# Uncast fp32 output stores on Sync's queue, and column halves for fewer weights and output blocks, in an attention plus soft-MoE kernel

## The chip, the cores and the metric

The kernel runs on one core of a Trainium2 chip. The metric is device time in microseconds of one execution, and less is better. Before the change the median of five runs is 190.15 us (189.98 to 190.43). The profile is that of one further execution, which took 189.8 us; its span, from the first to the last profiled instruction, is 188.0 us.

Five engines work beside each other, each in the order of its own program: PE (matrix multiply), DVE (vector), ACT (activation), POOL (GpSimd) and SP (Sync). Data moves between memory and the on-chip buffer SBUF by DMA, which an engine issues and 16 shared transfer engines carry out. A DMA that changes the data type goes through GpSimd's queue in this kernel.

## The reference

Attention with a sliding window for heads 0 to 3 and a dilated one for heads 4 to 7 gives `x` with 4608 rows and 512 columns. A soft mixture of experts follows:

```python
logits = x @ phi                                  # 4608 x 32
d = np.exp(logits - logits.max(0, keepdims=True)); d /= d.sum(0, keepdims=True) + 1e-09
slot_input = (d.T @ x).reshape(E, S_per_e, D)     # 8 experts, 4 slots each
for e in range(E):
    slot_out[e] = np.maximum(slot_input[e] @ w1[e], 0.0) @ w2[e]
c = np.exp(logits - logits.max(1, keepdims=True)); c /= c.sum(1, keepdims=True) + 1e-09
return (c @ slot_out.reshape(n_slots, D)).astype(np.float32)
```

`w1` is 8 x 512 x 1024 and `w2` is 8 x 1024 x 512, both fp32. Inputs and output are fp32; on the chip the arithmetic has fp16 operands and fp32 sums.

## The kernel before

The kernel has two parts. The first goes over the eight batches. For each it loads q, k and v, computes both kinds of attention, and from the result the exponentials of the logits (`ET`, 32 slots by 4608 rows, in four copies of which one lies on each quarter of the partitions) and the slot inputs. All of q, k, v and the weights are loaded by GpSimd's DMAs, which turn fp32 into fp16 on the way. The order of the instructions is written out by hand (`prologue`, `slot0`, `slot1`, `slot2`).

The weights' loads are issued between those of the attention: `weights` (L464) is called twice per batch. It issues w1 two at a time by `load_w1` (L194), and then w2 by `load_w2` (L198). `load_w2(e)` loads all of an expert's w2 in one DMA, whose pieces in memory are 8 KB (four rows of 512 fp32). `load_w2(e, half)` loads the left or right 256 columns in two DMAs, whose pieces are 1 KB. Experts 0, 1, 5 and 2 come whole; the experts of `HALVED` (3, 4, 6, 7) come as left halves first, then as right halves. Experts 5, 6 and 7 reuse buffers of the attention, so their loads wait until the last batches have let these go.

The second part begins when all batches are through. The slot inputs are multiplied by w1 (L620), go through ReLU and are transposed (L627 to L637). Then `slot_out` (L653) multiplies by w2, one half of the columns at a time, eight matmuls per expert and half, into `so[half]`, and after the last expert ACT copies the sum to `so_sb[half]` as fp16 (L665). `combine(half, pair)` (L669) makes two blocks of 128 output rows of one half of the columns: two matmuls of 256 columns each into a PSUM tile, then the scaling by `rrow` (one over the row sum of c), which moves the data to the fp16 tile `ot` in SBUF. Even pairs are scaled by ACT in two instructions (L685), odd pairs by DVE in one (L689). A GpSimd DMA then stores the tile, and turns fp16 to fp32 on the way (L695). There are 18 pairs of blocks for each half, thus 36 stores of 256 KB. The pool has 24 `ot` buffers (`NFIN // 2 + 6`), and PSUM has four for `combine`.

The main sequence (L700 to L710) takes the left half of all experts, the right half of the four whole ones, then the 18 left pairs; after pairs 5, 9 and 13 it puts in the right half of experts 3, 4 and 6, then that of 7, and then come the 18 right pairs. Since GpSimd issues stores as well as loads, all stores stand behind all loads in its queue. Sync issues nothing but the loads of the masks (L438) and of the identity matrix (L439) at the start; at the end it waits for every outstanding DMA, and a barrier over all engines (L742) closes the program.

Of the kernel before, what the change touches and what calls it, by code (L numbers as in the profile page):

```python
# [9 lines left out]
FP32 = mybir.dt.float32  # L10
FP16 = mybir.dt.float16
U32 = mybir.dt.uint32
AF = mybir.ActivationFunctionType
ALU = mybir.AluOpType
# [10 lines left out]
DMODEL = H * D  # L25
# [15 lines left out]
NFIN = N_ROWS // 128  # L41
UNITS = 7
NH = DMODEL // 2


def make_masks():
# [19 lines left out]
def kernel(  # L66
# [10 lines left out]
    nc = tc.nc  # L77
# [6 lines left out]
    consts = ctx.enter_context(tc.tile_pool(name="consts", bufs=1))  # L84
# [8 lines left out]
    ET = consts.tile([128, N_ROWS + 64], FP16, name="ET")  # L93
# [1 line left out]
    rcol = consts.tile([128, N_SLOTS], FP32, name="rcol")  # L95
    siTm = consts.tile([128, 4, E_EXP, N_SLOTS], FP16, name="siTm")
    rrow = consts.tile([128, NFIN], FP32, name="rrow")
    so_sb = [consts.tile([128, NH], FP16, name=f"so_sb{i}") for i in range(2)]

    w1_pool = ctx.enter_context(tc.tile_pool(name="w1p", bufs=1))  # L100
    w2a_pool = ctx.enter_context(tc.tile_pool(name="w2a", bufs=1))
# [21 lines left out]
    def slab_weights(e, tag, n):  # L123
        t = fix.tile([128, n], FP16, name=f"w2_{e}", tag=tag)
        w2t[e] = t[:, 0 : 8 * DMODEL].rearrange("p (c n) -> p c n", c=8)
# [68 lines left out]
    def load_w1(e, i):  # L194
        src = moe_w1[e].rearrange("(c p) f -> p c f", p=128)
        nc.gpsimd.dma_start(out=w1t[e][:, 2 * i : 2 * i + 2, :], in_=src[:, 2 * i : 2 * i + 2, :])  # L196

    def load_w2(e, half=None):  # L198
        if half is None:
            nc.gpsimd.dma_start(  # L200
                out=w2t[e].rearrange("p (h l) n -> p h (l n)", h=2),
                in_=moe_w2[e].rearrange("(h p l) n -> p h (l n)", h=2, l=4),
            )
            return
        src = moe_w2[e].rearrange("(h p l) n -> h p l n", h=2, l=4)
        c0 = NH * half
        for h in range(2):
            nc.gpsimd.dma_start(  # L208
                out=w2t[e][:, 4 * h : 4 * h + 4, c0 : c0 + NH], in_=src[h][:, :, c0 : c0 + NH]
            )  # L210
# [253 lines left out]
    def weights(b, g):  # L464
        if b < B - 2:
            if g == 1 or b > 0:
                load_w1(*next_w1.pop(0))
        elif b == B - 2:
            if g == 0:
                while next_w1:  # L470
                    load_w1(*next_w1.pop(0))
                load_w2(0)
                load_w2(1)
            else:
                slab_weights(5, "v2", V_SLAB)
                load_w2(5)
        elif g == 0:
            raw_pool.release()
            vs_pool.release()
            pool = tc.alloc_tile_pool(name="w2b", bufs=1, side="right")  # L480
            late_pools.append(pool)
            for e in (2, 3, 4):
                w2t[e] = pool.tile([128, 8, DMODEL], FP16, name=f"w2_{e}", tag=f"w2_{e}")
            slab_weights(6, "qk0", QK_SLAB)
            load_w2(2)
            for e in HALVED[:3]:
                load_w2(e, 0)
        else:
            slab_weights(7, "v0", V_SLAB)
            load_w2(7, 0)  # L490
            for e in HALVED:
                load_w2(e, 1)

    HALVED = (3, 4, 6, 7)
    late_pools = []

    def slot0(b):
        att, b1, b2, b3 = b < B, b - 1 >= 0 and b <= B, 2 <= b < B + 2, b + 1 < B
        if att:
            qk_dil(1, b, 1)  # L500
            emit_scores(b, 0)
            if b + 2 < B:
                load_qk(0, b + 2)
                load_qk(1, b + 2)
            weights(b, 0)
# [28 lines left out]
    def slot1(b):  # L534
        att, b1, b3 = b < B, 1 <= b <= B, b + 1 < B
        if b3:
            qk_plain(0, b + 1)
        if att:
            emit_scores(b, 1)
            if b + 2 < B:  # L540
                load_v(b + 2)
            weights(b, 1)
            emit_av(b, "p", 0)
            emit_norm(b, "p", 0)
        if b1:
            back_xT_dil(b - 1, 0)
        if b3:
            qk_plain(1, b + 1)
        if att:
            emit_av(b, "p", 1)  # L550
            emit_norm(b, "p", 1)
        if b1:
            back_xT_dil(b - 1, 1)
# [35 lines left out]
    xT_pool.release()  # L589
    x_pool.release()  # L590
    h_pool = tc.alloc_tile_pool(name="hp", bufs=1)
    out_pool = tc.alloc_tile_pool(name="outp", bufs=NFIN // 2 + 6)


    psum_so = tc.alloc_tile_pool(name="psum_so", bufs=1, space=bass.MemoryType.PSUM)
# [2 lines left out]
    for g in range(4):  # L598
# [8 lines left out]
        out=diag,  # L607
        in0=UT[:, 0:4, :].rearrange("p c (e s) -> p c e s", e=E_EXP),
# [6 lines left out]
    for fc in range(2):  # L615
        for g in range(2):
            for dc in range(4):
                for j in range(4):
                    e = 4 * g + j
# [4 lines left out]
                        start=(g == 0 and dc == 0),  # L624
                        stop=(g == 1 and dc == 3),
# [13 lines left out]
    for blk in range(NFIN):  # L639
# [4 lines left out]
            start=True,  # L644
            stop=True,
# [2 lines left out]
    psum_e.release()  # L648

    so = [psum_so.tile([128, NH], FP32, name=f"so{i}", tag=f"so{i}") for i in range(2)]  # L650
    ORDER = (0, 1, 5, 2) + HALVED

    def slot_out(half, experts):  # L653
        for e in experts:
            for c in range(8):
                g, j, a = e // 4, e % 4, c % 4
                nc.tensor.matmul(
                    so[half][32 * a : 32 * a + 32, :],
                    hTm[2 * g + c // 4][:, c % 4, 32 * j : 32 * j + 32],
                    w2t[e][:, c, NH * half : NH * half + NH],  # L660
                    start=(e == ORDER[0] and c < 4),
                    stop=(e == ORDER[-1] and c >= 4),
                )
        if experts[-1] == ORDER[-1]:
            nc.scalar.copy(out=so_sb[half], in_=so[half])  # L665

    psum_f = tc.alloc_tile_pool(name="psum_f", bufs=4, space=bass.MemoryType.PSUM)

    def combine(half, pair):  # L669
        fp = psum_f.tile([128, 2, NH], FP32, name=f"f{half}_{pair}", tag="f")  # L670
        r0 = 256 * pair
        for k in range(2):
            nc.tensor.matmul(  # L673
                fp[:, k, :],
                ET[:, r0 + 128 * k : r0 + 128 * k + 128],
                so_sb[half],
                start=True,
                stop=True,
                skip_group_check=True,
            )  # L680
        ot = out_pool.tile([128, 2, NH], FP16, name=f"ot{half}_{pair}", tag="ot")
        if pair % 2 == 0:
            for k in range(2):
                blk = 2 * pair + k
                nc.scalar.activation(  # L685
                    out=ot[:, k, :], in_=fp[:, k, :], func=AF.Copy, scale=rrow[:, blk : blk + 1]
                )
        else:
            nc.vector.tensor_tensor(  # L689
                out=ot,  # L690
                in0=fp,
                in1=rrow[:, 2 * pair : 2 * pair + 2, None].broadcast_to([128, 2, NH]),
                op=ALU.mult,
            )
        nc.gpsimd.dma_start(  # L695
            out=out[r0 : r0 + 256, NH * half : NH * half + NH].rearrange("(k p) n -> p k n", k=2),
            in_=ot,
        )

    with tc.manual_schedule(engines=None):  # L700
        slot_out(0, ORDER)
        slot_out(1, ORDER[:4])
        at = {5: 0, 9: 1, 13: 2}
        for pair in range(NFIN // 2):
            combine(0, pair)
            if pair in at:
                slot_out(1, (HALVED[at[pair]],))
        slot_out(1, HALVED[3:])
        for pair in range(NFIN // 2):
            combine(1, pair)  # L710
    psum_f.release()
    psum_so.release()
# [34 lines left out]
```

The softmax here doesn't subtract the row's maximum and nothing guards it: scores larger than these inputs give would overflow.

## Time and profile before

| What | Value |
|---|---|
| median of 5 runs | 190.15 us |
| profiled execution, and its span | 189.8 us, 188.0 us |
| PE busy | 124.0 us (66%) |
| DVE busy | 103.2 us (55%) |
| ACT busy | 87.9 us (47%) |
| GpSimd busy | 109.9 us (58%) |
| read from memory | 62.20 MB |
| written to memory | 9.44 MB |
| time of DMAs on the chain that ended last | 64% of the span |
| GpSimd's issuing of the 36 stores | 25.2 us, 706 ns each |
| ACT, scaling of 128 x 256 | 36 times, 479 ns each |
| DVE, scaling of 128 x 512 | 18 times, 690 ns each |
| PE, one combine matmul of 256 columns | 72 times, 323 ns mean in the last stage |

Busy time is the time in which an engine had an instruction at work. The profile's row "DMA" gives, for each fortieth of the span, the mean busy share of the 16 transfer engines in tenths; "GB/s" is what they moved, counted in bytes as written at the destination. A load that reads 4 bytes and writes 2 therefore shows half of what it reads. DMA shares over 1 in an answer about a stretch of time mean that transfer records overlap on one engine. The chain of waits goes back from the last instruction, at each step to what released it.

### The profile page before, as it was taken

How to read it: one execution, taken by the hardware profiler on the slowest of the kernel's cores; microseconds unless marked ns; L12 is line 12 of the kernel's file. 1: busy time of each engine (PE TensorE's matmuls, PEld its weight loads, DVE VectorE, ACT ScalarE, POOL GpSimd, SP SyncE). 2: the span in 40 equal slices, each digit the busy share in tenths (PEclk: the TensorE clock that was granted, in tenths of full speed). 3: DMA queues.
4: the chain of work that ended last, by engine and by line, in shares of the span. 5: the costliest groups of instructions: out<-in, count | busy, mean ns of one | idle time of the engine just before them, and what ended most of it. 6: DMA issues, size and time to landing. Idle time of an engine off the chain costs nothing.

```text
span 188.0 us, 5331 instructions
## 1 busy us (share of the span) xinstructions
PE 124.0 (66%) x2324; PEld 77.5 (41%) x2324; DVE 103.2 (55%) x229; ACT 87.9 (47%) x163; POOL 109.9 (58%) x143
## 2 busy tenths in 40 slices
PE   2151068999996698696599499997783398760000
PEld 0031035747665356265258158573532164530000
DVE  3683708798999289589179566560420048471000
ACT  2031056776961773961764755943020059680000
POOL 7759673966944934934942575211125536699970
PEclk9999999999999699999579889998599669697555
DMA  5999999999999999999999999999999999999991
GB/s 112 193 179 209 188 203 192 213 202 193 212 204 192 212 205 189 212 203 184 212 207 189 212 211 214 215 216 213 210 196 198 195 196 266 349 355 385 383 384 23
DMA packets 52328, 41.02 MB, mean 218 GB/s; under 512 B 20944, under 2 KB 43088, under 8 KB 52304
## 3 DMA queue, kind: packets, MB, share of 16 engines
q0 software_dynamic: 52016, 40.41, 133.3%
q8 instruction: 18, 0.29, 0.6%
q1 hardware_dynamic: 288, 0.27, 0.6%
q14 instruction: 6, 0.05, 0.1%
HBM read 62.20 MB, written 9.44 MB: 381 GB/s over the span
## 4 chain that ended last, share of the span: by engine, by line
DMA 64%; PE 15%; POOL 7%; issue 5%; ACT 4%; DVE 3%; POOLq 0%; ACTq 0%; DVEq 0%
DMA w<-in_moe_w_dram 36%; DMA vsa<-in_v_dram 15%; DMA v<-in_v_dram 8%; DMA raw<-in_q_dram 3%; POOL out_dram L695 3%; PE f L673 2%; DMA out_dram<-ot 2%; PE sa L264 2%; ACT p L275 2%; PE sb L253 2%; PE lg L383 2%; PE sa L253 1%; POOL v L160 1%; PE o_p L315 1%; DVE ot L689 1%
## 5 line engine op out<-in xcount | busy, mean ns | idle before, releaser
L253 PE MATMUL sa<-masks,ident 128*128 128x288 f16 (+2 forms) x48 | 14.7, 393 | 22.1 <-ACT p L275 18.5
L275 ACT ACTIVATE p<-sa 128x576 f16<-128x576 f32 (+2 forms) x24 | 19.6, 817 | 20.1 <-PE sb L264 19.9
L695 POOL DMA_DIRECT2D out_dram<-ot x36 | 25.2, 706 | 6.2 <-ACT ot L685 4.9
L208 POOL DMA_DIRECT2D w<-in_moe_w_dram x16 | 11.8, 740 | 24.8 <-DMA w<-in_moe_w_dram 20.1
L217 DVE STREAM_TRANSPOSE qk<-raw 128x576 uint32<-128x576 uint32 x16 | 20.0, 1249 | 7.1 <-DMA raw<-in_q_dram 6.0
L253 PEld LDWEIGHTS <-ident 128*128 128x128 f16 x96 | 9.9, 110 | 33.9 <-issue 28.2
L315 PEld LDWEIGHTS <-p 128*128 128x128 f16 (+2 forms) x448 | 17.6, 105 | 14.2 <-issue 9.6
L226 DVE STREAM_TRANSPOSE qk<-raw 128x320 uint32<-128x320 uint32 (+1 forms) x32 | 21.6, 679 | 0.3
L689 DVE TENSOR_TENSOR ot<-f,rrow 128x512 f16<-128x512 f32 x18 | 12.1, 690 | 17.0 <-PE f L673 16.1
L176 ACT COPY v<-vsa 128x1024 f16<-128x1024 f16 x8 | 8.4, 1045 | 26.5 <-DMA vsa<-in_v_dram 26.5
L275 ACT ACTIVATE p<-sb 128x576 f16<-128x576 f32 (+2 forms) x24 | 19.5, 813 | 0.0
L336 DVE RECIPROCAL rc_p<-o_p 96x6 f32<-96x6 f32 x32 | 5.8, 181 | 24.2 <-PE o_p L315 23.8
L264 PE MATMUL sa<-qk 32*128 32x96 f16 (+2 forms) x448 | 16.3, 216 | 4.2 <-DVE qk L217 4.2
L264 PEld LDWEIGHTS <-qk 32*128 32x128 f16 x896 | 12.7, 103 | 14.6 <-issue 9.9
L337 DVE TENSOR_TENSOR xp<-o_p,rc_p 96x384 f16<-96x384 f32 x32 | 17.7, 553 | 1.3
L383 PE MATMUL lg<-xTd,phi 128*128 128x288 f16 x32 | 18.2, 658 | 0.0
L315 PE MATMUL o_p<-v,p 128*128 128x65 f16 (+1 forms) x192 | 13.1, 211 | 5.1 <-POOL v L192 4.8
L264 PE MATMUL sb<-qk 32*128 32x96 f16 (+2 forms) x448 | 16.4, 217 | 0.0
L196 POOL DMA_DIRECT2D w<-in_moe_w_dram x16 | 11.4, 712 | 8.5 <-DMA raw<-in_k_dram 3.1
L685 ACT ACTIVATE ot<-f,rrow 128x256 f16<-128x256 f32 x36 | 14.2, 479 | 3.6 <-PE f L673 3.0
L253 PE MATMUL sb<-masks,ident 128*128 128x288 f16 (+2 forms) x48 | 14.8, 397 | 0.5 <-ACT p L275 0.3
L337 DVE TENSOR_TENSOR xd<-o_d,rc_d 128x448 f16<-128x448 f32 (+1 forms) x24 | 14.5, 602 | 0.8
(76 smaller groups left out, 239.1 us busy)
## 6 DMA issues: line engine op xcount, KB each, us to landing
out_dram<-ot POOLq DMA_DIRECT2D x36, 256.0 KB, 4.4
w<-in_moe_w_dram POOLq DMA_DIRECT2D x16, 512.0 KB, 15.8
w<-in_moe_w_dram POOLq DMA_DIRECT2D x4, 1024.0 KB, 24.6
w<-in_moe_w_dram POOLq DMA_DIRECT2D x16, 256.0 KB, 10.6
raw<-in_q_dram POOLq DMA_DIRECT2D x7, 576.0 KB, 12.2
raw<-in_k_dram POOLq DMA_DIRECT2D x7, 576.0 KB, 14.4
v<-in_v_dram POOLq DMA_DIRECT2D x8, 288.0 KB, 13.9
vsa<-in_v_dram POOLq DMA_DIRECT2D x8, 256.0 KB, 13.4
```

What stands on the lines that cost most here:

```text
L208: nc.gpsimd.dma_start(out=w2t[e][:, 4 * h : 4 * h + 4, c0 : c0 + NH], in_=src[h][:, :, c0 : c0 + NH])
L217: nc.vector.transpose(out=dst, in_=src)
L226: nc.vector.transpose(out=o, in_=i)
L253: nc.tensor.matmul(sps[h // 2][:, h % 2, 0:n], ident, bias, start=True, stop=False, skip_group_check=True,)
L264: nc.tensor.matmul(sps[h // 2][:, h % 2, c0 : c0 + w], kt_[32 * h : 32 * h + 32, k0 : k0 + 128, tt], qt_[32 * h : 32 * h + 32, q0 : q0 + w ...
L275: nc.scalar.activation(out=pt, in_=sps[ab][:, :, 0:n], func=AF.Exp, scale=SCALE)
L315: nc.tensor.matmul(o[p0 : p0 + np_, n, :], l, rr, start=(k == 0), stop=(k == len(jobs) - 1), skip_group_check=True,)
L337: nc.vector.tensor_tensor(out=x.rearrange("p t (h d) -> p (t h) d", h=4)[0:nq, u0:u1, :], in0=o[0:nq, 0:n, 0:D], in1=rc[0:nq, 0:n, None].b ...
L383: nc.tensor.matmul(lp, phi4[:, kc].rearrange("p c s -> p (c s)"), rhs, start=(kc == 0), stop=(kc == 3))
L685: nc.scalar.activation(out=ot[:, k, :], in_=fp[:, k, :], func=AF.Copy, scale=rrow[:, blk : blk + 1])
L689: nc.vector.tensor_tensor(out=ot, in0=fp, in1=rrow[:, 2 * pair : 2 * pair + 2, None].broadcast_to([128, 2, NH]), op=ALU.mult,)
L695: nc.gpsimd.dma_start(out=out[r0 : r0 + 256, NH * half : NH * half + NH].rearrange("(k p) n -> p k n", k=2), in_=ot,)
```

## The change

Four things change.

- Expert 3's w2 is loaded whole, after expert 2's. `HALVED` becomes (4, 6, 7), and `ORDER` is (0, 1, 5, 2, 3) and then `HALVED`. The right half of five experts, where it was four, is multiplied before the first `combine`.
- Only the first 20 of 36 blocks (`NSPLIT`) are made in column halves. The other 16 are made by a new function, `combine_full`, in full rows of 512 columns: per block one matmul of 512 columns, the first of a pair scaled by ACT, the second by DVE, and one store of 512 KB per pair. These eight pairs stand between the 10 left pairs and the 10 right ones. They have three buffers of their own.
- The tiles that hold outputs in SBUF are fp32. There are 10 `ot` buffers.
- All stores are issued by Sync, without a change of type. `so_sb` becomes one tile for both halves.

```diff
+NSPLIT = 20
-    so_sb = [consts.tile([128, NH], FP16, name=f"so_sb{i}") for i in range(2)]
+    so_sb = consts.tile([128, DMODEL], FP16, name="so_sb")
...
             load_w2(2)
-            for e in HALVED[:3]:
+            load_w2(3)
+            for e in HALVED[:2]:
                 load_w2(e, 0)
...
-    HALVED = (3, 4, 6, 7)
+    HALVED = (4, 6, 7)
...
-    out_pool = tc.alloc_tile_pool(name="outp", bufs=NFIN // 2 + 6)
+    out_pool = tc.alloc_tile_pool(name="outp", bufs=NSPLIT // 2)
...
-    ORDER = (0, 1, 5, 2) + HALVED
+    ORDER = (0, 1, 5, 2, 3) + HALVED
...
-            nc.scalar.copy(out=so_sb[half], in_=so[half])
+            nc.scalar.copy(out=so_sb[:, NH * half : NH * half + NH], in_=so[half])
...
-        ot = out_pool.tile([128, 2, NH], FP16, name=f"ot{half}_{pair}", tag="ot")
+        ot = out_pool.tile([128, 2, NH], FP32, name=f"ot{half}_{pair}", tag="ot")
...
-        nc.gpsimd.dma_start(
+        nc.sync.dma_start(
             out=out[r0 : r0 + 256, NH * half : NH * half + NH].rearrange("(k p) n -> p k n", k=2),
             in_=ot,
         )
 
+    def combine_full(pair):
+        r0 = 256 * pair
+        ot = out_pool.tile([128, 2, DMODEL], FP32, name=f"of_{pair}", tag="of", bufs=3)
+        for k in range(2):
+            blk = 2 * pair + k
+            fp = psum_f.tile([128, DMODEL], FP32, name=f"f_{blk}", tag="f")
+            nc.tensor.matmul(fp, ET[:, 128 * blk : 128 * blk + 128], so_sb, start=True, stop=True)
+            if k == 0:
+                nc.scalar.activation(
+                    out=ot[:, k, :], in_=fp, func=AF.Copy, scale=rrow[:, blk : blk + 1]
+                )
+            else:
+                nc.vector.tensor_scalar(
+                    out=ot[:, k, :],
+                    in0=fp,
+                    scalar1=rrow[:, blk : blk + 1],
+                    scalar2=None,
+                    op0=ALU.mult,
+                )
+        nc.sync.dma_start(
+            out=out[r0 : r0 + 256, :].rearrange("(k p) n -> p k n", k=2), in_=ot
+        )
+
     with tc.manual_schedule(engines=None):
         slot_out(0, ORDER)
-        slot_out(1, ORDER[:4])
-        at = {5: 0, 9: 1, 13: 2}
-        for pair in range(NFIN // 2):
+        slot_out(1, ORDER[:5])
+        at = {3: 0, 7: 1}
+        for pair in range(NSPLIT // 2):
             combine(0, pair)
             if pair in at:
                 slot_out(1, (HALVED[at[pair]],))
-        slot_out(1, HALVED[3:])
-        for pair in range(NFIN // 2):
+        slot_out(1, HALVED[2:])
+        for pair in range(NSPLIT // 2, NFIN // 2):
+            combine_full(pair)
+        for pair in range(NSPLIT // 2):
             combine(1, pair)
```

More of the change, by code (lines that the diff above doesn't have):

```diff
@@ L675, in combine @@
                 ET[:, r0 + 128 * k : r0 + 128 * k + 128],
-                so_sb[half],
+                so_sb[:, NH * half : NH * half + NH],
                 start=True,
```

## The prediction

> **What bounds the kernel now.** I read the page's slices first, then the rates of single stretches, then the chain of waits over the last 40 us, then the last semaphores.
>
> ```profile
> DMA  5999999999999999999999999999999999999991
> GB/s 112 193 179 209 188 203 192 213 202 193 212 204 192 212 205 189 212 203 184 212 207 189 212 211 214 215 216 213 210 196 198 195 196 266 349 355 385 383 384 23
> q0 software_dynamic: 52016, 40.41, 133.3%
> ```
>
> The transfer engines are full from the first slice to the last but one, while the compute engines idle more and more. The rate counts bytes as written. A load reads fp32 and writes fp16, so 196 to 216 GB/s of it are 392 to 432 GB/s read; a store writes fp32, so its 384 is the wide side already. Nearly all of it is in one software queue, GpSimd's. The stretches (columns: engines' busy time, clock, DMA share, GB/s last):
>
> ```profile
> 125.00:135.00 10.00, 7.61 (x136) 4.85 (x137) 3.46 (x13) 2.95 (x8) 1.70 (x3) 0.76 1.07 215
> 140.00:155.00 15.00, 8.72 (x123) 5.21 (x124) 2.51 (x6) 3.51 (x9) 7.20 (x10) 0.77 1.45 196
> 166.00:174.00 8.00, 1.82 (x13) 1.05 (x11) 2.79 (x5) 3.19 (x9) 8.00 (x13) 0.83 1.90 386
> 174.00:182.00 8.00, 0.00 (x0) 0.00 (x0) 0.00 (x0) 0.00 (x0) 8.00 (x12) 0.50 1.89 383
> ```
>
> The first is full w2 loads (8 KB read in one piece), the second column-half loads (1 KB pieces): the halves cost 9% of the rate. The last two are stores of 1 KB pieces. The chain at the turn from loads to stores:
>
> ```profile
> 150.08 10.42 DMA w<-in_moe_w_dram
> 160.50 0.04 issue
> 160.54 0.32 PE so L657 x4
> 160.86 0.02 issue
> 160.88 0.38 ACT so_sb L665
> 161.26 0.04 issue
> 161.31 3.16 PE f L673 x14
> ```
>
> The last load lands at 160.50. The stores that follow land at 185.33, where Sync's longest semaphore wait ends (182.0 + 3.325):
>
> ```profile
> L742 SPq EVENT_SEMAPHORE  x5: 27/28/3325, 182.0 to 185.5; - x5
> L742 SPq DRAIN  x2: 7/7/7, 185.6 to 185.7; - x2
> L742 POOLq DRAIN  x1: 6764/6764/6764, 180.5 to 180.5; - x1
> ```
>
> 36 stores x 262,144 B / 384 GB/s = 24.6 us, and 160.50 + 24.6 = 185.1. So the end is: loads, then stores, with almost nothing between. After it, Sync is through its waits at 185.7, but GpSimd's drain holds the final barrier until 187.3 (180.5 + 6.76); the end comes 0.75 later.
>
> **The change, part by part.**
>
> *Expert 3 loaded whole.* One load of 1,048,576 B written at 215 GB/s is 4.88 us; four halves at 196 are 5.35. Gain **0.47**: loads would end at 160.03. But the first half of the columns now waits for all of expert 3: 4.88 stand ahead of it where two halves of 1.34 each stood, so it is complete 2.2 us later. This row
>
> ```profile
> 149.84 2.11 PE L657 MATMUL so<-w,hTm 128*32 128x256 f16 x36 [0.92 <-DMA w<-in_moe_w_dram]
> ```
>
> moves to 152.05, and gets 8 matmuls more, because expert 3's second half is now done before the first combine (8 x 2.11/36 = 0.47). GpSimd's first store was issued at 153.72; Sync's comes at 153.72 + 2.2 + 0.5 = 156.4. This delay costs nothing as long as loads fill the engines, until about 160. The other DMAs keep their order; three fewer issues of 0.74 us on GpSimd are free, since the loads are throttled by earlier landings, not by GpSimd.
>
> *Stores by Sync, uncast.* The 25.2 us of GpSimd issuing go. Sync's two issues before took 0.34 and 0.43 us for 128 rows; a store has 256 row pieces. At 0.43 it keeps ahead of the 0.68 us that a store takes on the engines; if issue doubled to 0.86, the last ten stores would lag by 10 x 0.18 = 1.8. I take zero, by the nearer figure. The bytes written are the same; the bytes read from SBUF double, to as many as are written. No fp32-to-fp32 store is in this trace. The nearest rows are loads which read 392 GB/s in 1 KB pieces and stores which write 384: each side alone carries what is wanted of both, so I take 384 for a 1 KB store. Bounds: 1 us better (392, GpSimd's 0.70 us cadence gone) to 4 us worse (a 15% loss where both sides are full).
>
> Here a rule stands against hoping for more. The Trainium skill, "DMA: Bandwidth & Descriptors", section "Issuing engines are not separate DMA queues", says that a second issuing engine saves sequencer time only. By it the move to Sync is worth nothing in rate. The trace, however, prices something besides rate: the drain. GpSimd's last DMA is now a w2 load, so its drain is over long before the end, and the barrier waits for Sync alone: 187.3 - 185.7 = **1.6** gained. By the rule alone 0, by the row 1.6; I take the row, with 0 as the other bound (Sync's own drain, 7 ns with nothing in flight, might behave like GpSimd's).
>
> *Sixteen blocks stored in full rows.* Pieces are 2 KB. From the two load rates, one engine's piece of 1 KB takes 16 x 1024 B / 392 GB/s = 41.8 ns, one of 8 KB 16 x 8192 / 430 = 304.8; so 37.6 ns per KB and 4.2 ns per piece. A 2 KB piece is 79.4 against 83.6: 5% faster, 404 GB/s. Eight stores of 524,288 B: 8 x 1.30 = 10.4 instead of 16 x 0.68 = 10.9. Gain **0.5** (bounds 0 and 1).
>
> *Order and cover.* Only 10 half stores, 6.8 us of transfer, now stand between the first half and the full rows. Before, stores sat behind loads in one queue. Now they are in another queue. The skill's same page, "Queues, rings and completion order", says each engine takes turns between queues packet by packet. No stretch here shows two busy queues. By first-in order the last load lands at 160.0; by turns it shares from 157.4 (first store's data: issue 156.4 plus about 1.0, an estimate, half of what the masks' 2.7 us landing has beyond its 0.6 of moving) and lands as late as 162.7. Then PE 0.32, ACT 0.38, one combine matmul (about 0.6 with waits), one ACT evacuation of 512 columns (0.479 for 256; 0.650 for 576 in another row, so about 0.65 to 0.7), issue and 1.0: the first full row reaches the engines at 166.0. The loads left (2.7) and the 6.8 us of half stores fill them from 157.4 to 166.9. So it is just covered, by 0.9. If it weren't, each us too late would cost one.
>
> *Three buffers for full rows.* A buffer's round: evacuation 0.7, waits 0.1, issue to data 1.0, data 1.3, landing 0.4: 3.5 us, against 3 x 1.3 = 3.9 of transfer. Slack 0.4; behind the waiting evacuations stand, in ACT's and DVE's order, the last ten half rows. The fourth to eighth store wait: five rounds. Bounds 0 and 3; I take **+0.5**. The last ten stores have ten free buffers and evacuate at about 0.5 us each, faster than 0.68.
>
> *Evacuation itself.* fp32 output: ACT reads fp32 from PSUM as before, and there is no cover to lose: both engines finish well inside the transfers (14.2 us ACT, 12.1 DVE, over 25).
>
> **Sum against the profiled run.** 185.3 - 0.47 - 0.5 + 0.5 = 184.8 for the last landing; + 0.4 for Sync's checks + 0.75 = 186.0 span, against 188.0. The profiled run took 189.8, 1.8 outside the span, so 187.8; the median stands 0.35 above that run: **188.1 us**.
>
> **Rivals.**
>
> *A, the seam opens or the drain stays.* The queues share badly, so that the last load comes after the half stores, and full rows start 1 to 2 us late; or Sync's drain takes the place of GpSimd's 1.6. Either leaves 189.5 to 190.2. For: the margin of 0.9 and the slack of 0.4 are thin. Against: whichever queue goes first, the same bytes remain.
>
> *B, slower: uncast stores run below 384 GB/s.* Place: the 23 us of stores. What I gain without it is 2.1 us, so it decides from 9% loss of rate, about 350 GB/s; at 330 GB/s stores take 27.8 instead of 23.9, giving 192.0. For: fp32 on both sides was never at work here, and small-piece descriptors now come from another generator. Against: the DMA share of 1.9 shows overlapped packets, so reading and writing already go side by side.
>
> *C, better.* No bubbles and 392 GB/s: 188.1 - 0.5 - 0.5 = 187.1.
>
> **Chances.** Forecast 0.42, C 0.18, A 0.13, B 0.27. A measurement of this kernel tells 0.2% (0.4 us) from nothing. A is mostly inside or just under that; so faster 0.61, same 0.09, slower 0.30. Range 186.4 to 192.0: C below, most of B above; without B it would be 186.4 to 189.9.
>
> **What would show it.** GpSimd's drain ends before 170 and the last Sync wait is within 1.2 us of the end. Half stores hold 380 or more, full rows 400 or more. w2's last landing lies between 160 and 163, and no slice in between falls under 350 GB/s. I am wrong if the stores' plateau is under 360, if ACT waits for landings of the full rows with the engines idle, or if the drain is still last.

## The result, and the profile after

The changed kernel takes 189.16 us in the median of 21 runs (188.1 to 190.06); the kernel before took 190.21 in the median of 40 runs on the same chips. The ratio is 0.9945, with a 95% interval of 0.993 to 0.996: about 1.05 us faster, where 2.05 were forecast. The profiled run took 189.47 us, its span is 187.7. It lies 0.3 above its median and the profiled run before 0.4 below its own, so the two profiles differ by less than the medians do.

First the page's slices of the changed kernel, then its queues:

```profile
DMA  5999999999999999999999999999999999997996
GB/s 111 188 181 208 186 204 191 204 203 187 214 206 188 214 208 186 213 207 185 211 205 190 212 210 214 213 217 216 213 212 200 194 196 206 355 377 265 378 342 228
q0 software_dynamic: 40384, 30.97, 107.1%
q1 hardware_dynamic: 7904, 9.71, 14.8%
```

GpSimd's queue q0 has kept the loads, and the stores are in Sync's q1. Two things are new at the end. Slice 37 of the rate falls to 265 between 377 and 378, and the last full slice holds 342 where the kernel before had 384. Stretches of the last 30 us (columns as before: busy time of PE, its weight loads, DVE, ACT, GpSimd; clock, DMA share, and GB/s last):

```profile
157.00:158.00 1.00, 1.00 (x12) 0.27 (x11) 0.91 (x2) 0.78 (x2) 0.00 (x0) 0.50 0.83 115
164.00:169.50 5.50, 0.89 (x3) 0.20 (x3) 0.52 (x1) 0.08 (x1) 0.00 (x0) 0.96 1.04 377
169.50:171.50 2.00, 1.01 (x2) 0.25 (x2) 1.20 (x2) 1.16 (x2) 0.00 (x0) 0.50 0.29 109
171.50:178.00 6.50, 5.37 (x20) 2.67 (x20) 4.28 (x7) 4.64 (x11) 0.00 (x0) 0.50 1.02 379
179.00:186.00 7.00, 0.32 (x2) 0.00 (x0) 0.80 (x2) 0.77 (x2) 0.00 (x0) 0.74 1.01 341
```

The same first stretch in the kernel before:

```profile
157.00:158.00 1.00, 0.66 (x11) 0.23 (x9) 1.00 (x2) 1.00 (x4) 0.70 (x1) 1.00 1.69 287
```

At 157 part of the transfer engines seem to have no load left before the first store's data comes: the DMA share is 0.83 (1.69 before) and the rate 115 GB/s, while the last load still lands at 161.02. From 169.5 to 171.5 the transfer engines are mostly idle in the midst of the full rows (share 0.29). The last half rows run at 341. This drop of the rate is called the dip below. The timeline of ACT names who waits in it:

```profile
162.82 1.26 ACT L710 ACTIVATE of<-f,rrow 128x512 f32<-128x512 f32 x2
169.75 0.69 ACT L710 ACTIVATE of<-f,rrow 128x512 f32<-128x512 f32 x1 [5.67 <-DMA out_dram<-of]
171.03 0.69 ACT L710 ACTIVATE of<-f,rrow 128x512 f32<-128x512 f32 x1 [0.60 <-DMA out_dram<-of]
```

The fourth full row waits 5.67 us for the landing of the first, whose buffer it takes. At the end, the view of the closing line shows the drains:

```profile
L769 POOLq DRAIN  x3: 51/98/11849, 150.6 to 187.4; - x3
L769 SPq DRAIN  x3: 7/7/7, 186.8 to 187.2; - x3
```

GpSimd's long drain starts at 150.6 and is over at 162.4; Sync's takes 7 ns. The last store lands at 186.64, and the span ends 1.04 us later (2.7 before). So in these two profiles the landing came 1.3 us later than in the kernel before and the end 1.7 us sooner after it.

### The profile page after: what moved, and what is told of

It reads as the page before. It is cut to its first block, busy times and chain, and to the rows that moved or that the text cites. A ratio compares the mean times of both kernels' runs of the same rounds, so it can differ in the third digit from the quotient of the medians.

```text
span 187.7 us, 5272 instructions
## 1 busy us (share of the span) xinstructions
PE 124.5 (66%) x2308; PEld 74.4 (40%) x2308; DVE 103.2 (55%) x229; ACT 86.8 (46%) x155; POOL 82.6 (44%) x104
## 4 chain that ended last, share of the span: by engine, by line
DMA 60%; PE 19%; ACT 6%; DVE 4%; issue 3%; POOL 2%; ACTq 0%; SPq 0%; DVEq 0%; POOLq 0%
DMA vsa<-in_v_dram 23%; DMA w<-in_moe_w_dram 21%; DMA v<-in_v_dram 8%; DMA out_dram<-of 5%; PE lg L384 4%; DMA raw<-in_q_dram 4%; ACT p L276 3%; PE sa L265 3%; PE sb L254 2%; PE f L675 2%; DVE of L714 2%; PE o_p L316 1%; ACT xTp L358 1%; PE u L425 1%; PE sa L254 1%
## 5 line engine op out<-in xcount | busy, mean ns | idle before, releaser
L254 PE MATMUL sa<-masks,ident 128*128 128x288 f16 (+2 forms) x48 | 13.7, 370 | 23.7 <-ACT p L276 20.2
L316 PEld LDWEIGHTS <-p 128*128 128x128 f16 (+2 forms) x448 | 16.8, 102 | 14.7 <-issue 10.0
L209 POOL DMA_DIRECT2D w<-in_moe_w_dram x12 | 8.9, 744 | 27.4 <-DMA w<-in_moe_w_dram 25.4
L691 DVE TENSOR_TENSOR ot<-f,rrow 128x512 f32<-128x512 f32 x10 | 6.8, 690 | 16.7 <-PE f L675 16.6
L197 POOL DMA_DIRECT2D w<-in_moe_w_dram x16 | 11.3, 709 | 7.3 <-DMA raw<-in_k_dram 3.3
L254 PE MATMUL sb<-masks,ident 128*128 128x288 f16 (+2 forms) x48 | 13.8, 374 | 0.9 <-ACT p L276 0.5
L659 PE MATMUL so<-w,hTm 128*32 128x256 f16 x128 | 7.8, 351 | 9.2 <-DMA w<-in_moe_w_dram 8.4
L161 POOL DMA_DIRECT2D v<-in_v_dram x8 | 9.6, 1197 | 8.2 <-PE rd L365 2.8
```

What stands on the lines that cost most here:

```text
L161: nc.gpsimd.dma_start(out=vt[32:128, :, :, 0:D], in_=v[b, 0:4].rearrange("h (t a) d -> a (h t) d", t=NT))
L209: nc.gpsimd.dma_start(out=w2t[e][:, 4 * h : 4 * h + 4, c0 : c0 + NH], in_=src[h][:, :, c0 : c0 + NH])
L254: nc.tensor.matmul(sps[h // 2][:, h % 2, 0:n], ident, bias, start=True, stop=False, skip_group_check=True,)
L316: nc.tensor.matmul(o[p0 : p0 + np_, n, :], l, rr, start=(k == 0), stop=(k == len(jobs) - 1), skip_group_check=True,)
```

## The experiments

The runs whose names begin with the same letter went to one chip, with the kernel before beside them. The chips differ (the kernel before takes 190.0 to 190.38), so runs of different letters are compared by the ratio. All medians and intervals:

| Run | Median, us | Ratio to before (95%) |
|---|---|---|
| changed kernel | 189.16 | 0.9945 (0.993 to 0.996) |
| e1_pool_fp32 | 193.98 | 1.0201 (1.0177 to 1.0226) |
| e2_pool_fp16 | 191.26 | 1.0061 (1.004 to 1.0081) |
| e3_w3_whole | 189.57 | 0.9975 (0.9963 to 0.9986) |
| e4_all_halves_sync | 188.95 | 0.9939 (0.9917 to 0.9961) |
| f1_of_bufs4 | 188.20 | 0.9887 (0.9869 to 0.9905) |
| f2_of_4kb | 188.01 | 0.9885 (0.9864 to 0.9906) |
| f3_late_sync | 190.68 | 1.0021 (1.0007 to 1.0036) |
| f4_cast_mix | 190.12 | 0.9988 (0.9975 to 1.0) |
| g1_w3_halves | 190.59 | 1.0009 (0.9992 to 1.0026) |
| g2_split16 | 187.95 | 0.9868 (0.9845 to 0.9892) |
| g3_cast_bufs8 | 189.50 | 0.9954 (0.9937 to 0.9971) |
| g4_split12 | 188.15 | 0.9869 (0.9842 to 0.9897) |

### Is it the queue or the missing cast?

The first suspect was the plateau of 341 GB/s in the last half rows. Both stores of the changed kernel go back to GpSimd, with fp32 tiles (e1) or fp16 tiles (e2):

```diff
-        nc.sync.dma_start(
+        nc.gpsimd.dma_start(
```

and in e2, besides,

```diff
-        ot = out_pool.tile([128, 2, NH], FP32, ...
+        ot = out_pool.tile([128, 2, NH], FP16, ...
-        ot = out_pool.tile([128, 2, DMODEL], FP32, ...
+        ot = out_pool.tile([128, 2, DMODEL], FP16, ...
```

> The changed kernel with both stores issued by GpSimd, still fp32 and uncast. Open: why 1 KB stores run at about 343 GB/s at the end of the changed kernel where 384 was forecast. Theory Q (the queue costs it, 48 ns per 1 KB piece on Sync's against 42 on GpSimd's): the last ten half stores run at 380 GB/s or more, the last landing comes 1.5 us earlier than with Sync, GpSimd's drain takes 1.6 back: 189.3 us. Theory U (fp32 on both sides costs it): the plateau stays at about 343, and with the drain back the time is 190.7.

> The changed kernel with both stores issued by GpSimd from fp16 tiles, so that only the whole expert 3 and the full rows in the middle are left of the change. Q and U both: half stores at 384 GB/s, full rows at 400. Q: the same time as the kernel with fp32 stores from GpSimd. U: 1.4 us faster than that one. In numbers: 189.2 us, that is 0.5 for expert 3 and 0.5 for the full rows under the kernel before.

Neither theory had the times: 193.98 and 191.26 us, where 189.2 was expected of e2. The stall of the full rows accounts for about 2 us of it in e2 (g3, below). The plateaus decide. The last half rows of e1, then of e2:

```profile
180.00:188.00 8.00, 1.04 (x5) 0.41 (x3) 1.38 (x2) 1.39 (x4) 5.75 (x9) 0.50 0.99 320
```

```profile
180.00:185.50 5.50, 0.00 (x0) 0.00 (x0) 0.45 (x1) 0.18 (x1) 4.33 (x7) 0.50 1.96 397
```

Same queue, same shapes, same order: 320 GB/s uncast and 397 with the cast. So theory Q falls: on one queue, fp32 tiles without a cast cost the rate. Sync's queue is not the slow one: uncast it has 341, 6% more than GpSimd's. The cast and the source's size can't be told apart here, since an fp16 tile also halves the bytes read from SBUF. The column before the rate shows a trait: the DMA share is 1.96 with the cast, so the records of two packets overlap on each engine, and 0.99 without. The whole kernel is 2.7 us slower uncast (191.26 to 193.98).

Nor does Sync's issuing set the 341. In the changed kernel it issued the last ten stores 0.77 us apart, but each landed about 3.3 us after its issue, so several were always waiting, and the DMA share stayed at 1.01.

Beside the changed kernel, e1 differs by the issuing engine alone, and so shows the drain by itself:

```profile
L769 POOLq DRAIN  x3: 95/184/7673, 183.7 to 192.1; - x3
```

It starts at 183.7 and takes 7.67 us, until 191.4, though the last store lands at 189.86. The span ends 2.68 us after that landing, where the changed kernel's ends 1.04 after its own: 1.64 of the 4.9 us between the two kernels. The rest lies before the landing.

The other end of the same question: 36 blocks in halves, all by Sync.

```diff
-NSPLIT = 20
+NSPLIT = 36
```

> The changed kernel with all 36 blocks in column halves (NSPLIT 36), stored by Sync in fp32. If 1 KB pieces on Sync's queue cost 0.77 us per 256 KB, the 16 halves that replace 8 full rows take 12.3 us instead of 10.6: 1.7 slower than the changed kernel, 190.9 us, and the plateau is 343 GB/s throughout. If the low rate belongs only to the last ten stores, 0.5 slower: 189.7.

A miss both ways. The rate is low throughout:

```profile
162.00:184.00 22.00, 6.92 (x48) 3.73 (x45) 7.18 (x11) 8.75 (x23) 0.00 (x0) 0.70 1.04 349
```

Yet 188.95 us is no slower than the changed kernel (0.9939 against 0.9945). The full rows, which do run faster, must lose what they gain. That pointed to the dip.

### The whole expert 3, alone

The kernel before, with expert 3's w2 loaded in one DMA, the five whole experts ahead of the first combine, and nothing else:

```diff
-            for e in HALVED[:3]:
+            load_w2(3)
+            for e in HALVED[:2]:
                 load_w2(e, 0)
-    HALVED = (3, 4, 6, 7)
+    HALVED = (4, 6, 7)
```

> The kernel before with expert 3 loaded whole, and nothing else. By the load rates 0.47 us less: 189.7 us. If the later completion of the first column half starves the stores, no gain or a loss: 190.2 to 190.7.

Ratio 0.9975: 0.48 us, as expected (0.27 to 0.70 by the interval). But from 156 to 159 us the rate falls here too, since the first store is issued at 157.75 where it was 153.72:

```profile
156.00:159.00 3.00, 3.00 (x34) 1.85 (x31) 2.57 (x4) 3.00 (x9) 1.25 (x2) 0.85 0.92 124
```

And the way was not the expected one: the last load lands at 160.76, where it landed at 160.50 before and 160.03 was forecast. Where the 0.48 comes from isn't shown.

### The three buffers

The changed kernel with four buffers for the full rows, the only edit:

```diff
-        ot = out_pool.tile([128, 2, DMODEL], FP32, name=f"of_{pair}", tag="of", bufs=3)
+        ot = out_pool.tile([128, 2, DMODEL], FP32, name=f"of_{pair}", tag="of", bufs=4)
```

> The changed kernel with four buffers for the full rows where it had three; there is room for no more. Open: whether the dip to 55 and 225 GB/s at 170 to 172 us, where the fourth full row waits for the first one's landing, costs time. Theory S (it does, since the engines that ran dry can't catch up): the fourth store is issued by 167, the dip shrinks by about 1.3 us of transfer, 188.0 us. Theory L (only the engine that lands last counts, and it has no gap): no change, 189.2.

Theory S holds: 188.20 us, 1.1 less than the changed kernel (0.9887 against 0.9945). The same stretches with four buffers:

```profile
169.50:171.50 2.00, 0.61 (x2) 0.26 (x2) 0.82 (x2) 0.78 (x2) 0.00 (x0) 0.50 1.03 387
179.00:185.00 6.00, 0.00 (x0) 0.00 (x0) 0.14 (x1) 0.00 (x0) 0.00 (x0) 0.78 1.04 347
```

The dip is gone (387 for 109), although ACT still waits for a landing, now before the fifth full row:

```profile
170.16 0.69 ACT L710 ACTIVATE of<-f,rrow 128x512 f32<-128x512 f32 x1 [5.06 <-DMA out_dram<-of]
```

So it is not the wait that costs, but what is left in the queue during it. The last full row lands at 179.06, as in the changed kernel (178.99); all that is gained comes after it. The mean rate of the last half rows has hardly moved (347 for 341), but they now land 0.68 us apart where they landed 0.76 apart. Theory L looked at landings alone: in the changed kernel full rows land every 1.2 to 1.4 us right through the dip. A landing tells of the last engine to finish. My reading is that the engines that were ahead ran dry in the dip and lost their lead, and in the last ten stores all were late together. In e4, which has no such dip, the same turn comes late and without a change of rate: stores land 0.67 to 0.71 us apart from 164 to 179.7, and 0.75 to 0.81 apart after that (352 and 345 GB/s). But the records don't name the engine of a packet, so the lead itself isn't shown, only that in the dip most engines were idle while stores were still to land.

In GpSimd's queue with the cast the stall can be had alone, by eight fp16 buffers in e2's kernel (`bufs=3` becomes `bufs=8`):

> The changed kernel with both stores by GpSimd from fp16 tiles, and eight buffers for the full rows, so that none waits for a landing. It isolates the stall in GpSimd's queue: the earlier one with three buffers lost 0.93 us at the fourth and 0.92 at the seventh full row. So 191.3 - 1.85 = 189.4 us, with the last landing at 184.8 and the drain's end 2.7 after it. If the stall had another cause, 191.3.

189.50 us, as expected (last landing 185.2, a little later than 184.8). Three buffers cost 2.0 us there, by the ratios (1.0061 and 0.9954). The rate of its full rows, 2 KB pieces with the cast, is 414 GB/s, then of its last half rows 396:

```profile
166.00:175.00 9.00, 4.04 (x24) 2.11 (x22) 5.27 (x9) 5.51 (x13) 6.99 (x10) 0.86 1.48 414
177.00:182.00 5.00, 0.00 (x0) 0.00 (x0) 0.00 (x0) 0.00 (x0) 3.12 (x5) 0.50 1.95 396
```

It keeps its drain: last landing 185.2, end of span 187.9, again 2.7 us. With four buffers and Sync (f1) they are 185.8 and 186.9.

### The price of a piece

Four buffers again, and the layout of the full rows changes: a partition holds two neighbouring rows, so the store's piece is 4 KB.

```diff
-            nc.tensor.matmul(fp, ET[:, 128 * blk : 128 * blk + 128], so_sb, start=True, stop=True)
+            nc.tensor.matmul(fp, ET[:, r0 + k : r0 + 256 : 2], so_sb, start=True, stop=True)
...
-            out=out[r0 : r0 + 256, :].rearrange("(k p) n -> p k n", k=2), in_=ot
+            out=out[r0 : r0 + 256, :].rearrange("(p k) n -> p k n", k=2), in_=ot
```

The row sums `rs` are taken from the same columns of ET.

> The same with four buffers, and the full rows laid out so that each partition holds two neighbouring rows and stores one piece of 4 KB in place of two of 2 KB (weights taken from every second column of ET, row sums to match). Theory P (an uncast store pays about 10 ns for each piece, which a cast one hides, and then 37.7 ns per KB): a 4 KB piece takes 161 ns, 407 GB/s, where 2 KB runs at 383; 8 stores gain 0.6 us, 187.4. Theory B (uncast stores are bound by bytes, whatever the piece): the plateau of the full rows stays at 383, 188.0.

The full rows of this run, then its last half rows:

```profile
166.00:169.50 3.50, 0.00 (x0) 0.00 (x0) 0.08 (x1) 0.10 (x1) 0.00 (x0) 1.00 1.03 410
177.00:183.50 6.50, 0.00 (x0) 0.00 (x0) 0.29 (x1) 0.45 (x2) 0.00 (x0) 0.76 1.03 348
```

410 GB/s, where 407 was expected: theory P. On Sync's queue an uncast store of 1, 2 and 4 KB pieces runs at 341 to 349, 379 and 410 GB/s. The time missed: it is 188.01 us, which four buffers alone had within the intervals (188.20), where theory P had 187.4.

### Whose turn it is

Expert 3 in halves again, in that last version, with the right halves of experts 3, 4 and 6 after pairs 3, 6 and 9:

```diff
-            load_w2(3)
-            for e in HALVED[:2]:
+            for e in HALVED[:3]:
                 load_w2(e, 0)
-    HALVED = (4, 6, 7)
+    HALVED = (3, 4, 6, 7)
```

> The version with four buffers and 4 KB pieces, with expert 3 back in column halves: the load part of the change undone, the rest kept. By the load rates 0.47 us slower, 188.5. Rival: expert 3 whole delays the first store by 2.2 us, and the transfer engines that are through with their loads run dry at 156 to 159 us (down to 110 GB/s as written), which the stores can't make up; then the halves cost nothing or gain: 187.5 to 188.0, with no dip at 157.

Both were wrong by far: 190.59 us, 2.4 more (1.0009 against 0.9885). The chain of waits of this run, at the end of the loads, and its rate afterwards:

```profile
151.29 14.12 DMA w<-in_moe_w_dram
165.41 0.04 issue
165.45 0.43 PE so L658 x4
```

```profile
157.00:164.00 7.00, 1.93 (x26) 0.83 (x19) 1.51 (x3) 1.64 (x4) 0.00 (x0) 0.73 1.19 325
164.00:169.00 5.00, 3.08 (x11) 1.20 (x11) 1.50 (x2) 2.10 (x4) 0.00 (x0) 0.50 0.42 144
```

Stores start at 154.65 here, 2.1 us sooner than in that version, and share the engines with the loads for as long as there are loads. The last load lands at 165.41 (160.81 in that version) and the first full row is issued at 168.19; the tenth half store had been issued at 162.15, so little is left to move: 144 GB/s for 5 us. So in this kernel with two queues a first half that is complete early does harm, and the whole expert 3, which delays it, is worth far more than by its load rate.

### Two versions with the last stores on Sync

In f3 the kernel before has fp32 tiles and Sync for its last four stores; f4 is the kernel of g3 with the same edit:

```diff
-        nc.gpsimd.dma_start(
+        late = half == 1 and pair >= LATE
+        (nc.sync if late else nc.gpsimd).dma_start(
```

> The kernel before with only its last four stores changed: fp32 tiles, uncast, by Sync. It measures the drain by itself: GpSimd's drain should be over before the last landing, so that the end comes 1.05 us after it where it came 2.7 after. The four stores at 0.77 instead of 0.68 cost 0.35. 190.15 - 1.65 + 0.35 = 188.85 us. If the drain is no cost of GpSimd's queue but of any last DMA: 190.5.

> A version put together from the findings: expert 3 whole, the changed kernel's order and full rows, but fp16 tiles stored with the cast by GpSimd (395 GB/s for 1 KB pieces, 415 for 2 KB), eight buffers for the full rows so that none waits, and the last four stores in fp32 by Sync, so that no drain follows. Against the kernel before: 0.45 for expert 3, 0.5 for the full rows, 1.6 for the drain, less 0.35 for the four stores: 187.95 us. If the stall of the full rows was not a matter of buffers: 189.5.

Both missed, and the drain stayed (2.6 us after the last landing in f3, 2.1 in f4). I had taken the last four stores in the program for the last on the chip. In their own queue they don't stand behind GpSimd's: in f3 Sync issued them from 169.74 on and they landed by 179.44, while GpSimd's stores went on landing to 186.72. So these runs don't measure the drain by itself. They show that the program's order is not kept between two queues. While both queues store, the mean rate in f3 is 359 GB/s:

```profile
172.00:175.00 3.00, 0.00 (x0) 0.00 (x0) 0.00 (x0) 0.00 (x0) 3.00 (x5) 0.63 1.47 359
```

### How many blocks in halves

From the version with 4 KB pieces: 16 blocks in halves with five full-row buffers, and 12 with six (right halves of experts 4 and 6 after pairs 2 and 4).

```diff
-NSPLIT = 20
+NSPLIT = 16
```

> The same version (expert 3 whole, 4 KB pieces) with 16 blocks in halves where there were 20, so two more pairs in full rows, with five buffers for these and eight for the halves. If full rows now cost only their pieces, two stores of 4 KB pieces (1.29 us each) replace four of 1 KB (0.77 each): 1.0 less, 187.0. If 8 left pairs don't cover the time until the first full row, a dip at 163 to 165 us and 188.0 or more.

> As the version with 16 blocks in halves, but with 12: four pairs more in full rows than in the changed kernel, six buffers for these and six for the halves. Cover lost: six left stores are 4.6 us of transfer from 157.4, so they end before the first full row reaches the engines at about 165. Gain 2.0 from pieces, loss 2 to 3 from the gap: 188.0 to 189.0. If cover is not needed, 186.0.

g2 is at 187.95 us and g4 at 188.15, which the intervals don't tell apart from f2. So the gain of 1.0 us that was expected of g2 did not come, though it has no dip at 162 to 165 us; g4, with the least cover, has the gap that was expected of it. First g2, then g4:

```profile
162.00:165.00 3.00, 2.67 (x11) 0.91 (x10) 2.65 (x4) 2.87 (x5) 0.00 (x0) 1.00 1.05 371
```

```profile
162.00:165.00 3.00, 2.91 (x8) 1.03 (x8) 1.75 (x3) 2.00 (x4) 0.00 (x0) 0.58 0.52 182
```

The lowest ratio is g2's, 0.9868: 1.3% faster than the kernel before and 0.8% faster than the changed one, but no faster than f1, f2 and g4 beyond the intervals.

## Why the prediction was right and wrong

The step that failed is the sizing of "Three buffers for full rows": +0.5 was forecast and about 1.1 measured. The second is the rate of uncast stores, forecast at the cast stores' 384 GB/s with no cost and measured at 341 to 349. Of its three signs of being wrong two came: a stores' plateau under 360, and ACT waiting for landings with the transfer engines idle. The third, the drain coming last, did not.

- **Expert 3 whole, 0.47.** The number is right alone (e3: 0.48), the way to it is not shown: the last load came no sooner (160.76 in e3, 160.50 before), so the agreement is luck in part. That the later first store "costs nothing as long as loads fill the engines, until about 160" was wrong: the rate had fallen to 124 GB/s from 156 to 159 (e3). With two queues the delay even guards the last load (g1).
- **The drain, 1.6.** Right: from the last landing to the end 2.7 us with GpSimd (before, g3, e1) and 1.04 with Sync, whose drain took 7 ns. Between e1 and the changed kernel, which differ by the issuing engine alone, it is 1.64.
- **Uncast stores at 384 GB/s.** Wrong as a mean rate: 341 to 349. I had read the DMA share of 1.9 as proof that reading and writing go side by side; it belongs to stores with a cast. Little of it reached the end: f1, uncast throughout, is 1.3 us faster than g3, cast throughout (0.9887 against 0.9954), where the drain alone would give 1.6 to 1.7. That leaves a loss of 0.3 to 0.4, which is within the intervals. By the forecast's rule a second issuing engine changes no rate; of uncast stores Sync's ran at 341 and GpSimd's at 320.
- **Full rows, 0.5.** 379 GB/s instead of 404 as uncast; with the cast 414. With buffers enough and the cast (g3 against e3, 0.9954 to 0.9975) they gain 0.4, on two chips and hardly beyond the intervals.
- **Taking turns.** Not visible in the changed kernel: its last load landed at 161.02, and at 160.5 to 161.1 in the runs with all in GpSimd's queue and expert 3 whole (e1, e2, e3, g3). It shows in g1, where stores start earlier: 165.41. The cover of the gap held in the changed kernel, and failed in g1 and g4.
- **Three buffers, +0.5.** This is the term that decided. It measured 1.1 (f1). I summed a round of 3.5 us against 3.9 of transfer. From the first full row's issue at 164.06 its landing took 5.6 us, since it stood behind half stores. A later round took 3.9, with no slack: landing 170.93, evacuation until 171.8, issue at 171.87, landing 174.82. And I treated 16 engines as one stream: in the dip most of them were idle (share 0.29) while two full rows had yet to land.

In differences of measured ratios, times 190.2: expert 3 -0.48, full rows (cast, and buffers enough) -0.40, from there to uncast on Sync with four buffers -1.27, three buffers instead of four +1.10; together -1.05. In the forecast these are -0.47, -0.5, -1.6 and +0.5, together about -2.05. Each of these differences carries an interval of 0.2 to 0.5 us, so only their order of size is firm. Of the missing 1.0 us, about 0.6 is the buffers' term; the rest is within the noise of the uncast rate's and the full rows' terms.

What stays open: why an uncast packet doesn't overlap with the next; whether the cast or the smaller source makes the other store faster; and why, with four buffers, half stores land every 0.68 us while the mean rate is 347 GB/s, which would be 0.76.

## What to carry to other kernels

Count buffers so that the transfers already queued outlast the wait for a landing, and look for the dip in the rate, not at the spacing of landings: here three buffers instead of four cost 1.1 us while landings went on evenly. Moving stores to a second queue gives up the order that one queue gave for nothing: stores that start early can hold up the last loads, and what needs these loads comes later (g1: 4.6 us). The queue that is drained at the end is part of the time: between the last landing and the end lay 2.7 us with GpSimd and 1.0 with Sync.

## What was not expected of the hardware

A store that casts fp16 to fp32 on the way was faster than one that moves fp32 as it is: 397 against 320 GB/s on GpSimd's queue with pieces of 1 KB, though the uncast one does less to the data. It does read twice the bytes from SBUF. Uncast on Sync's queue, longer pieces made up for it: 341 to 349, 379 and 410 GB/s for 1, 2 and 4 KB.
